# A spectral mix with its bias added by GpSimd in SBUF instead of by PE in PSUM

## The chip, the cores and the metric

The kernel runs on one core of one Trainium2 chip. A core has five engines that run side by side, each through its own instructions in order: PE (TensorE, matmuls into PSUM), VectorE (DVE), ScalarE (ACT), GpSimd (POOL) and SyncE (SP, which here issues the DMAs). They wait for each other by semaphores. The metric is device time in microseconds (us), the median of the runs shown. GpSimd reaches SBUF only; PSUM is read by VectorE and ScalarE.

## The reference, cut to what matters

```python
batch, seq, dim = 8, 3136, 256
X = np.fft.rfft(x, axis=1)                       # along the sequence
Yr = X.real @ w_r - X.imag @ w_i + b_r           # the mix, with its bias
Yi = X.real @ w_i + X.imag @ w_r + b_i
Yr = np.sign(Yr) * np.maximum(np.abs(Yr) - 0.01, 0.0)    # soft threshold, Yi alike
y = np.fft.irfft(Yr + 1j * Yi, n=seq, axis=1)
h = np.maximum(y @ w_in, 0.0)                    # then a gated feed-forward net, d_ff = 1024
gate = 1 / (1 + np.exp(-conv3(h, conv_w)))       # a 3-tap convolution along the sequence
out = (h * gate) @ w_out
```

The change touches the two lines of the mix alone: where b_r and b_i are added.

## The kernel before, in words

The sequence of 3136 is taken as 56 x 56, so that each Fourier transform is two rounds of small matmuls with tables of sines and cosines. The program has two halves. The first one (to about 580 us) makes the transform, the mix, the threshold and the first half of the inverse transform. The second one (the rest) ends the inverse transform (stage 4) and runs the feed-forward net; its instructions stand in the same order before and after the change.

The first half works on 56 groups, 7 for each of the 8 sequences, each of 4 frequencies u. One turn of its loop, for `it`, records:

- stage 2 for group it (`stage2`): eight matmuls of the second transform round, each of which PE runs as two. ScalarE copies and casts the result (tiles d and fh), VectorE makes the rest (d, fl). Numbers are kept in two parts, a high one rounded to PE's fast format (fh) and a low one (fl), so one product is three matmuls. The last piece, fl<-d,fh, reads d and fh, both in SBUF.
- the mix for group it - 1 (`mix`, named below). A complex product is made with three real products: a common one, and one for each of the two parts. The common product (ps_mx2) is copied to SBUF by ScalarE (p1, the profile's "p<-ps_mx"), and VectorE adds it to the other two (ps_mx0, ps_mx1) with four sums "v<-ps_mx,p" of 64 partitions, two per part. The threshold follows: ScalarE makes r from v, VectorE v from v and r ("v<-v,r"), ScalarE casts v to sh, and GpSimd makes the low part sl from v and sh.
- stage 3 for group it - 3 (`stage3`): 12 matmuls on sh and sl, a copy z by ScalarE and a store by SP.
- stage 1 for a later group: matmuls "ps_s<-xr,f", of which each group has two, and a copy a of each by ScalarE. For the last ten groups there is no stage 1 left.
- two pieces of background work on VectorE, which turns the feed-forward weights from double precision to two floats (the rows named win_ and wout_, later cw_): short ones with one tensor input, longer ones with two.

The bias before: two tiles, `ones` (0 but for rows 0 and 32, which are 1) and `bias` (0 but for row 0, the high part, and row 32, the low part). A matmul of `ones` with `bias` adds the bias to all 128 rows of an output. Each of the two parts has two column blocks k, so a group has four such products beside its 36 others.

The order on each engine is not the order of the code. A scheduler takes the recorded instructions, runs its own model of the engines' times, and fixes one order for each engine at build time; on the chip each engine goes through that order. The tiles that matter have few buffers: the three ps_mx tiles have one each, so that a group's products can only start when the sums of the group before have read them; sl has one, so that GpSimd waits for stage 3 of the group before; p1, v and sh have two.

Of the kernel before, what the change touches and what calls it, by code (L numbers as in the profile page):

```python
# [9 lines left out]
F32 = mybir.dt.float32  # L10
F32R = mybir.dt.float32r
I32 = mybir.dt.int32
AF = mybir.ActivationFunctionType
ALU = mybir.AluOpType
# [3 lines left out]
B, S, D, FF = 8, 3136, 256, 1024  # L18
# [6 lines left out]
UG = 4  # L25
NG = U // UG
JC = 4
P = 128
# [67 lines left out]
def spectral_ffn_kernel(ctx: ExitStack, tc: tile.TileContext, x, w_r, w_i, b_r, b_i,  # L96
                        w_in, conv_w, w_out, fwd1, fwd2, inv1, inv2, out):
    nc = tc.nc
    K1, K2 = 2 * R, 2 * SP
# [16 lines left out]
    with ExitStack() as ab:  # L116
        stg = ab.enter_context(tc.tile_pool(name="stg", bufs=1))
# [4 lines left out]
        cmx = ab.enter_context(tc.tile_pool(name="cmx", bufs=1))  # L122
# [5 lines left out]

        f1 = c1.tile([K1, P], F32, name="f1")[:, 0:K1]
        t2 = c1.tile([K1, U, K2], F32, name="t2")  # L130
        ones = cmx.tile([P, K2], F32R, name="ones")
        bias = cmx.tile([P, 2, D], F32R, name="bias")
        cmx.tile([P, 96], F32, name="pad")
        wmix_hi = cmx.tile([P, NT, 3, D], F32R, name="wmix_hi")
        wmix_lo = cmx.tile([P, NT, 3, D], F32R, name="wmix_lo")
# [3 lines left out]
        def split(dst_hi, dst_lo, src):  # L139
            nc.scalar.copy(dst_hi, src)  # L140
            nc.vector.tensor_tensor(dst_lo, src, dst_hi.bitcast(F32), op=ALU.subtract)
# [17 lines left out]

        def load_bias():  # L160

            nc.vector.memset(ones.bitcast(F32), 0.0)
            for k in (0, 32):
                nc.vector.memset(ones[k:k + 1].bitcast(F32), 1.0)
            nc.vector.memset(bias.bitcast(F32), 0.0)
            raw = stg.tile([1, 2, D], F32, name="b_raw")
            for k in range(2):
                nc.sync.dma_start(raw[:, k, :], (b_r, b_i)[k].partition_broadcast(1))
            split(bias[0:1], bias[32:33], raw)

        def load_inv1(g):
            raw = stg.tile([K2, UG, K1], F32, name="i1_raw", tag="raw", bufs=2)
# [126 lines left out]
        def mix(xs):  # L299


            fh, fl = xs
            ps = [psm.tile([K2, UG // 2, D], F32, name=f"ps_mx{c}") for c in range(3)]
            for c in (2, 0, 1):
                q = (1, 2, 0)[c]
                for k in range(UG // 2):
                    mm = [(ones, bias[:, c, :])] if c < 2 else []
                    for t in range(NT):
                        a = [f[:, t, c, 2 * k:2 * k + 2, :] for f in (fh, fl)]
                        mm += [(a[0], wmix_hi[:, t, q, :]), (a[0], wmix_lo[:, t, q, :]), (a[1], wmix_hi[:, t, q, :])]  # L310
                    for n, (lt, rh) in enumerate(mm):
                        nc.tensor.matmul(ps[c][:, k, :], lt, rh, start=(n == 0), stop=(n == len(mm) - 1))  # L312
            p1 = wk.tile([K2, UG // 2, D], F32, name="p1")
            nc.scalar.copy(p1, ps[2])
            v = wk.tile([K2, UG // 2, 2, D], F32, name="v")
            half = (slice(0, SP), slice(SP, K2))
            for c in range(2):
                for k in range(2):
                    src, dst = half[k], half[k if c == 0 else 1 - k]
                    nc.vector.tensor_tensor(v[dst, :, k, :], ps[c][src], p1[src], op=ALU.add)  # L320
            v = v.rearrange("p a b d -> p (a b) d")
            sh = wk.tile([K2, UG, D], F32R, name="sh")
            sl = wk.tile([K2, UG, D], F32R, name="sl", bufs=1)
            r = wk.tile([K2, UG, D], F32, name="r", bufs=1)
            nc.scalar.activation(r, v, AF.Relu, bias=mlam)  # L325
            thr = nc.vector.scalar_tensor_tensor(v, v, LAM, r, op0=ALU.add, op1=ALU.min)  # L326
            nc.scalar.copy(sh, v)
            SL_ENG.tensor_tensor(sl, v, sh.bitcast(F32), op=ALU.subtract)  # L328
            return sh, sl, thr
# [22 lines left out]
        p1 = NG  # L352
        load_f1()
        with tc.tile_pool(name="hx", bufs=1, reuse_waits="tile") as hx:
            xh = []
            for p in range(NG):
                xr, ld = load_x(hx, 0, p, parts=2 if p == 0 else 1, tag=f"hx{p}")
                xh.append(xr)
            with tc.issue_after(ld.ins):
                load_t2(0)  # L360
                load_mix()
                load_bias()
                st = stage1_head(xh)
        with tc.issue_after(st.ins):
# [3 lines left out]
            for i in range(2):  # L368
                a2s[i], ld = load_a2(*items[i])
        ab.enter_context(tc.issue_after(ld.ins))  # L370
        wkf, wk, cab, io = [ab.enter_context(tc.tile_pool(name=nm, bufs=n, reuse_waits="tile"))
                            for nm, n in (("wkf", 2), ("wk", 2), ("cab", 1), ("io", 2))]
# [7 lines left out]
        for it in range(n_it + 3):  # L380
            if it + 2 < n_it:
                a2s[it + 2], _ = load_a2(*items[it + 2])
            if it < n_it:
                xs[it] = stage2(items[it][1], a2s.pop(it))
            if it < NG:
                load_inv1(it)
                if it + 1 < NG:
                    load_t2(it + 1)
            if 0 <= it - 1 < n_it:
                ss[it - 1] = mix(xs.pop(it - 1))  # L390
            if 0 <= it - 3 < n_it:
                stage3(*items[it - 3], ss.pop(it - 3))
            while p1 < n_it and p1 < min(it + AHEAD, NG + 2 + it + it // 2):
                stage1(*items[p1])
                p1 += 1
            if WP0 <= it < n_it:
                with tc.issue_after(ss[it - 1][2].ins):
                    for _ in range(2 if it < LAST else 12):
                        next(background, None)


    def pool(name, bufs=1, **kw):
        return ctx.enter_context(tc.tile_pool(name=name, bufs=bufs, reuse_waits="tile", **kw))

    zio, y_a = pool("zio", 3), pool("y_a")
    wk, hp, io, y_b = pool("cwk"), pool("chp", 3), pool("cio"), pool("y_b")
# [135 lines left out]
```

## Time and profile before

| | |
|---|---|
| three runs | 1788.65, 1791.27, 1795.26 us |
| median | 1791.27 us |
| profiled execution, span | 1796.8 us |
| busy share of the span | PE 98%, VectorE 83%, ScalarE 69%, GpSimd 7% |
| first half of the program | to about 580 us, 56 groups |
| GpSimd in the first half | 56 instructions of 2.37 us |

The profiled execution is one more run of the same program; its span, from the first instruction to the last, is the only time of it that the page gives. It lies 5.5 us above the median.

How the rows read: a timeline row gives start, duration, engine, line, operation, tile written<-tiles read (buffer numbers left out), size, count and, in brackets, how long the engine stood idle before it and what ended the wait. A group row gives busy time and mean duration in ns, then idle time before the instructions and who ended it. A row of the table by stretch gives the stretch, its length, busy time and count of PE, PE's weight loads, VectorE, ScalarE and GpSimd, then the granted TensorE clock, the busy share of the DMA engines and GB/s. A row that describes one line's instructions gives minimum, median and maximum duration in ns.

### The profile page before, as it was taken

How to read it: one execution, taken by the hardware profiler on the slowest of the kernel's cores; microseconds unless marked ns; L12 is line 12 of the kernel's file. 1: busy time of each engine (PE TensorE's matmuls, PEld its weight loads, DVE VectorE, ACT ScalarE, POOL GpSimd, SP SyncE). 2: the span in 40 equal slices, each digit the busy share in tenths (PEclk: the TensorE clock that was granted, in tenths of full speed). 3: DMA queues.
4: the chain of work that ended last, by engine and by line, in shares of the span. 5: the costliest groups of instructions: out<-in, count | busy, mean ns of one | idle time of the engine just before them, and what ended most of it. 6: DMA issues, size and time to landing. Idle time of an engine off the chain costs nothing.

```text
span 1796.8 us, 29723 instructions
## 1 busy us (share of the span) xinstructions
PE 1761.6 (98%) x12320; PEld 1652.4 (92%) x12320; DVE 1484.6 (83%) x1733; ACT 1244.7 (69%) x1638; POOL 133.0 (7%) x60
## 2 busy tenths in 40 slices
PE   6999999999998999999999999999999999999999
PEld 2888989989998899999999999999999999999998
DVE  2787777787788688888888898888888888888887
ACT  2667667667665677777677777767777777767766
POOL 0122222222223000000000000000000000000000
PEclk8999999999999999999999999999999999999999
DMA  9777676676543311011011001101101111100001
GB/s 252 226 218 213 189 217 198 195 218 187 163 134 107 89 52 42 21 52 52 31 52 52 32 32 52 52 32 52 52 26 58 52 42 42 42 21 22 22 21 42
DMA packets 106810, 164.11 MB, mean 91 GB/s; under 512 B 8754, under 2 KB 85428, under 8 KB 106676
## 3 DMA queue, kind: packets, MB, share of 16 engines
q1 hardware_dynamic: 106676, 162.22, 30.2%
q8 instruction: 97, 1.59, 0.4%
q14 instruction: 37, 0.30, 0.1%
HBM read 85.13 MB, written 77.07 MB: 90 GB/s over the span
## 4 chain that ended last, share of the span: by engine, by line
PE 92%; DMA 3%; DVE 2%; ACT 1%; issue 1%; SPq 0%; ACTq 0%; DVEq 0%
PE acc L477 31%; PE ps_h L449 31%; PE ps_mx L312 12%; PE ps_s L430 5%; PE ps_s L288 5%; PE ps_s L253 4%; PE ps_s L338 4%; DVE v L320 1%; DMA wm_raw<-in_w_i_dram 1%; DMA i_raw<-in_inv_dram 1%; DMA t<-in_fwd_dram 1%; ACT r L325 0%; DMA xr<-in_x_dram 0%; DVE fl L294 0%; DMA sc<-a 0%
## 5 line engine op out<-in xcount | busy, mean ns | idle before, releaser
L477 PE MATMUL acc<-wout,gh 128*128 128x256 f32 x3136 | 567.4, 280 | 0.0
L449 PE MATMUL ps_h<-yh,win 128*128 128x450 f32 x1792 | 551.8, 368 | 1.3 <-ACT yh L436 1.2
L458 DVE SCALAR_TENSOR_TENSOR c<-h,cw,c 128x896 f32<-128x896 f32 x448 | 512.6, 1146 | 49.1 <-ACT c L456 48.1
L477 PEld LDWEIGHTS acc<-wout,gh 128*128 128x128 f32 x3136 | 493.7, 188 | 6.5
L477 PE MATMUL acc<-wout,gl 128*128 128x256 f32 x1568 | 437.6, 281 | 0.0
L451 ACT ACTIVATE h<-ps_h 128x900 f32<-128x900 f32 x224 | 207.5, 926 | 257.0 <-PE ps_h L449 256.9
L449 PEld LDWEIGHTS ps_h<-yh,win 128*128 128x128 f32 x1792 | 339.5, 189 | 27.6 <-ACT yh L436 1.4
L449 PE MATMUL ps_h<-yl,win 128*128 128x450 f32 x896 | 330.0, 368 | 0.7 <-DVE yl L437 0.7
L477 PEld LDWEIGHTS acc<-wout,gl 128*128 128x128 f32 x1568 | 293.7, 188 | 0.1
L464 DVE TENSOR_TENSOR gl<-c,gh 128x896 fp32r<-128x896 f32 x224 | 242.8, 1088 | 53.0 <-ACT gh L463 49.6
L460 DVE TENSOR_TENSOR c<-h,c 128x896 f32<-128x896 f32 x224 | 243.2, 1086 | 47.1 <-ACT c L459 46.7
L463 ACT CAST gh<-c 128x896 fp32r<-128x896 f32 x224 | 209.8, 942 | 49.3 <-DVE c L460 49.3
L459 ACT ACTIVATE c<-c 128x896 f32<-128x896 f32 x224 | 213.3, 952 | 26.4 <-DVE c L458 23.4
L312 PE MATMUL ps_mx<-wmix_hi,fh 128*128 128x256 f32 x672 | 210.0, 313 | 0.0
L312 PE MATMUL ps_mx<-wmix_hi,fl 128*128 128x256 f32 x672 | 189.3, 283 | 3.0 <-DVE fl L296 2.9
L312 PE MATMUL ps_mx<-wmix_lo,fh 128*128 128x256 f32 x672 | 189.2, 282 | 0.0
L449 PEld LDWEIGHTS ps_h<-yl,win 128*128 128x128 f32 x896 | 169.4, 189 | 12.1 <-DVE yl L437 1.0
L456 ACT ACTIVATE c<-h,cw 128x896 f32<-128x896 f32 x168 | 175.5, 1045 | 2.6
L328 POOL TENSOR_TENSOR sl<-v,sh 128x1024 fp32r<-128x1024 f32 x56 | 132.8, 2371 | 449.0 <-PE ps_s L338 382.2
L320 DVE TENSOR_TENSOR v<-ps_mx,p 64x512 f32<-64x512 f32 x224 | 154.0, 688 | 7.2 <-ACT fh L295 1.8
L326 DVE SCALAR_TENSOR_TENSOR v<-v,r 128x1024 f32<-128x1024 f32 x56 | 78.6, 1404 | 81.7 <-ACT r L325 81.6
L312 PEld LDWEIGHTS ps_mx<-wmix_hi,fh 128*128 128x128 f32 x672 | 127.0, 189 | 12.1 <-issue 11.9
(93 smaller groups left out, 2168.8 us busy)
## 6 DMA issues: line engine op xcount, KB each, us to landing
a<-sc SPq DMA_DIRECT2D x56, 448.0 KB, 5.4
sc<-z SPq DMA_DIRECT2D x56, 448.0 KB, 3.2
z<-sc SPq DMA_DIRECT2D x56, 448.0 KB, 3.9
xr<-in_x_dram SPq DMA_DIRECT2D x55, 448.0 KB, 4.2
out_dram<-o SPq DMA_DIRECT2D x27, 896.0 KB, 4.0
sc<-a SPq DMA_DIRECT2D x49, 448.0 KB, 4.4
sc<-ha SPq DMA_DIRECT2D x7, 448.0 KB, 5.5
win_bits<-in_moe_w_in_dram SPq DMA_DIRECT2D x4, 512.0 KB, 8.7
```

Source lines behind the costliest of these rows:

```text
L312: nc.tensor.matmul(ps[c][:, k, :], lt, rh, start=(n == 0), stop=(n == len(mm) - 1))
L320: nc.vector.tensor_tensor(v[dst, :, k, :], ps[c][src], p1[src], op=ALU.add)
L328: SL_ENG.tensor_tensor(sl, v, sh.bitcast(F32), op=ALU.subtract)
L449: nc.tensor.matmul(ps[:, a, 0:CH + 2], lt, rh, start=(n == 0), stop=(n == len(mm) - 1))
L451: nc.scalar.activation(h, ps[:, :, 0:CH + 2], AF.Relu)
L456: nc.scalar.mul(c, h[:, :, 0:CH], cw[:, 0, f:f + 1])
L458: nc.vector.scalar_tensor_tensor(c, h[:, :, k:k + CH], cw[:, k, f:f + 1], c, op0=ALU.mult, op1=ALU.add)
L459: nc.scalar.activation(c, c, AF.Sigmoid)
L460: nc.vector.tensor_tensor(c, h[:, :, 1:CH + 1], c, op=ALU.mult)
L463: nc.scalar.copy(gh, c)
L464: nc.vector.tensor_tensor(gl, c, gh.bitcast(F32), op=ALU.subtract)
L477: nc.tensor.matmul(acc[m // 2][:, m % 2, :], lt[:, sl], rh[:, f, :], start=(f == 0 and n == 0 and m % 2 == 0), stop=(f == NF - 1 and n == ...
```

## The change

The products with `ones` go. The bias is loaded into all 128 partitions as a plain float tile, and GpSimd makes two versions of the common product: p0 with b_r added, and p1, in place, with b_i added. The four sums on VectorE read p0 or p1 instead of p1 alone. The sums themselves, the three products and all that follows stay as they were.

```diff
-        ones = cmx.tile([P, K2], F32R, name="ones")
-        bias = cmx.tile([P, 2, D], F32R, name="bias")
+        bias = cmx.tile([P, 2, D], F32, name="bias")
...
         def load_bias():
-            nc.vector.memset(ones.bitcast(F32), 0.0)
-            for k in (0, 32):
-                nc.vector.memset(ones[k:k + 1].bitcast(F32), 1.0)
-            nc.vector.memset(bias.bitcast(F32), 0.0)
-            raw = stg.tile([1, 2, D], F32, name="b_raw")
             for k in range(2):
-                nc.sync.dma_start(raw[:, k, :], (b_r, b_i)[k].partition_broadcast(1))
-            split(bias[0:1], bias[32:33], raw)
+                nc.sync.dma_start(bias[:, k, :], (b_r, b_i)[k].partition_broadcast(P))
...
-                    mm = [(ones, bias[:, c, :])] if c < 2 else []
+                    mm = []
...
             p1 = wk.tile([K2, UG // 2, D], F32, name="p1")
             nc.scalar.copy(p1, ps[2])
+            p0 = wk.tile([K2, UG // 2, D], F32, name="p0", bufs=1)
+            pb = (p0, p1)
+            for c in range(2):
+                nc.gpsimd.tensor_tensor(pb[c], p1, bias[:, c:c + 1, :].to_broadcast([K2, UG // 2, D]), op=ALU.add)
...
-                    nc.vector.tensor_tensor(v[dst, :, k, :], ps[c][src], p1[src], op=ALU.add)
+                    nc.vector.tensor_tensor(v[dst, :, k, :], ps[c][src], pb[c][src], op=ALU.add)
```

The two DMAs of the bias keep their place in SP's queue, behind the mix's weights and ahead of the first stage-1 stores. Each now writes 128 rows of 1 KB.

The scheduler makes a new order of it. Three places follow, all from the 27th group of 56, one among many that are alike. (Lines below `load_bias` are numbered 7 less after the change, those behind the new adds 3 less.)

ScalarE, from one group's copy p1 to the next one's. Before:

```order
L314 COPY p1_3259<-ps_mx2_3218 128x512
L295 CAST fh_3193<-d_3195 128x2x256
L254 COPY a1_3177<-ps_s1_3181 112x512
L340 COPY z1_3286<-ps_s3_3273 112x1024
L325 ACTIVATE r_3268<-v_3261,small_82 128x1024
L254 COPY a1_3291<-ps_s1_3292 112x512
L291 COPY d_3305<-ps_s2_3306 128x256
L292 CAST fh_3303<-ps_s2_3306 128x512
L291 COPY d_3305<-ps_s2_3315 128x256
L292 CAST fh_3303<-ps_s2_3315 128x512
L327 CAST sh_3266<-v_3261 128x1024
L314 COPY p1_3369<-ps_mx2_3328 128x512
```

After:

```order
L307 COPY p1_3221<-ps_mx2_3184 128x512
L288 CAST fh_3159<-d_3161 128x2x256
L337 COPY z1_3251<-ps_s3_3238 112x1024
L247 COPY a1_3256<-ps_s1_3257 112x512
L322 ACTIVATE r_3233<-v_3226,small_82 128x1024
L284 COPY d_3270<-ps_s2_3271 128x256
L285 CAST fh_3268<-ps_s2_3271 128x512
L284 COPY d_3270<-ps_s2_3280 128x256
L285 CAST fh_3268<-ps_s2_3280 128x512
L324 CAST sh_3231<-v_3226 128x1024
L247 COPY a1_3256<-ps_s1_3260 112x512
L307 COPY p1_3330<-ps_mx2_3293 128x512
```

The two copies a of stage 1 moved: one now stands before r, the other between sh and the next p1. The activation r, the four instructions on d and fh, sh and the next p1 keep their order, and the cast of d (fh<-d) still comes right behind p1.

VectorE, from one threshold (v<-v,r) to the next. Before:

```order
L326 SCALAR_TENSOR_TENSOR v_3261<-v_3261,r_3268 128x1024
L194 TENSOR_SCALAR wout_e_3185<-wout_e_3185 128x512
L293 TENSOR_TENSOR d_3305<-ps_s2_3306,d_3305 128x256
L294 TENSOR_TENSOR fl_3304<-ps_s2_3306,fh_3303 128x512
L195 SCALAR_TENSOR_TENSOR wout_e_3185<-wout_bits_2518,wout_e_3185 128x512
L293 TENSOR_TENSOR d_3305<-ps_s2_3315,d_3305 128x256
L294 TENSOR_TENSOR fl_3304<-ps_s2_3315,fh_3303 128x512
L296 TENSOR_TENSOR fl_3304<-d_3305,fh_3303 128x2x256
L320 TENSOR_TENSOR v_3371<-ps_mx0_3326,p1_3369 64x2x256 x2
L320 TENSOR_TENSOR v_3371<-ps_mx1_3327,p1_3369 64x2x256 x2
L326 SCALAR_TENSOR_TENSOR v_3371<-v_3371,r_3378 128x1024
```

After:

```order
L323 SCALAR_TENSOR_TENSOR v_3226<-v_3226,r_3233 128x1024
L187 TENSOR_SCALAR wout_e_3151<-wout_e_3151 128x512
L286 TENSOR_TENSOR d_3270<-ps_s2_3271,d_3270 128x256
L287 TENSOR_TENSOR fl_3269<-ps_s2_3271,fh_3268 128x512
L286 TENSOR_TENSOR d_3270<-ps_s2_3280,d_3270 128x256
L287 TENSOR_TENSOR fl_3269<-ps_s2_3280,fh_3268 128x512
L188 SCALAR_TENSOR_TENSOR wout_e_3151<-wout_bits_2490,wout_e_3151 128x512
L289 TENSOR_TENSOR fl_3269<-d_3270,fh_3268 128x2x256
L317 TENSOR_TENSOR v_3335<-ps_mx0_3291,p0_3332 64x2x256 x2
L317 TENSOR_TENSOR v_3335<-ps_mx1_3292,p1_3330 64x2x256 x2
L323 SCALAR_TENSOR_TENSOR v_3335<-v_3335,r_3342 128x1024
```

The second piece of background work (a wout_e row here) moved from between the two halves of stage 2 to the place directly ahead of fl<-d,fh, which itself stands ahead of the four sums.

GpSimd, of which before only the rows of sl follow each other, after the change:

```order
L311 TENSOR_TENSOR p0_3223<-p1_3221,bias_115 128x512
L311 TENSOR_TENSOR p1_3221<-p1_3221,bias_115 128x512
L325 TENSOR_TENSOR sl_3119<-v_3113,sh_3118 128x1024
L311 TENSOR_TENSOR p0_3332<-p1_3330,bias_115 128x512
L311 TENSOR_TENSOR p1_3330<-p1_3330,bias_115 128x512
L325 TENSOR_TENSOR sl_3232<-v_3226,sh_3231 128x1024
```

The two adds of a group stand ahead of sl of the group before it. The second add overwrites p1, which the first one reads, so it waits for the first one's end.

## The prediction

> **What bounds the kernel now.** I read the busy shares first, then a table by stretch, then single groups of the mix stage on each engine, because the change touches that stage alone (about 50 to 580 us).
>
> ```profile
> PE 1761.6 (98%) x12320; PEld 1652.4 (92%) x12320; DVE 1484.6 (83%) x1733; ACT 1244.7 (69%) x1638; POOL 133.0 (7%) x60
> ...
> 20.00:50.00 30.00, 19.40 (x92) 13.59 (x93) 13.98 (x24) 11.65 (x24) 0.00 (x0) 0.72 1.01 266
> 300.00:400.00 100.00, 100.00 (x750) 89.61 (x749) 79.81 (x126) 70.65 (x121) 23.74 (x10) 1.00 0.71 214
> 500.00:600.00 100.00, 90.97 (x731) 88.80 (x730) 76.03 (x129) 61.17 (x88) 25.53 (x11) 0.96 0.48 134
> ```
>
> PE never rests in a mix stretch (100.00 of 100), VectorE has 20% free, ScalarE 29%, GpSimd 76%. The pace of one group is seen on PE, from one mix's first matmul to the next one's, and on GpSimd's single instruction:
>
> ```profile
> 299.95 0.37 PE L312 MATMUL ps_mx<-wmix_hi,fh 128*128 128x256 f32 x1
> ...
> 303.94 0.28 PE L312 MATMUL ps_mx<-bias,ones 128*128 128x256 f32 x1
> 304.06 0.28 PE L312 MATMUL ps_mx<-wmix_hi,fh 128*128 128x256 f32 x1
> ...
> 304.76 0.28 PE L312 MATMUL ps_mx<-bias,ones 128*128 128x256 f32 x1
> ...
> 309.56 0.37 PE L312 MATMUL ps_mx<-wmix_hi,fh 128*128 128x256 f32 x1
> 326.44 2.36 POOL L328 TENSOR_TENSOR sl<-v,sh 128x1024 fp32r<-128x1024 f32 x1 [7.24 <-PE ps_s L338]
> 336.05 2.38 POOL L328 TENSOR_TENSOR sl<-v,sh 128x1024 fp32r<-128x1024 f32 x1 [7.24 <-PE ps_s L338]
> ```
>
> A group takes 9.61 us on both. Matmuls are pipelined: a row shows 0.28 us, but from bias to bias seven starts lie 0.82 us apart, 0.117 us each. That is the price of a bias product, not its duration.
>
> **What is removed.** Four of 40 matmuls per group, 224 in all.
>
> ```profile
> L312 PE MATMUL ps_mx<-bias,ones 128*128 128x256 f32 x224 | 65.2, 291 | 1.4 <-DVE v L320 0.8 <-DVE ha L270 0.6
> L320 DVE TENSOR_TENSOR v<-ps_mx,p 64x512 f32<-64x512 f32 x224 | 154.0, 688 | 7.2 <-ACT fh L295 1.8 <-ACT p L314 1.0 <-issue 0.4
> L328 POOL TENSOR_TENSOR sl<-v,sh 128x1024 fp32r<-128x1024 f32 x56 | 132.8, 2371 | 449.0 <-PE ps_s L338 382.2 <-ACT sh L327 66.8
> L460 DVE TENSOR_TENSOR c<-h,c 128x896 f32<-128x896 f32 x224 | 243.2, 1086 | 47.1 <-ACT c L459 46.7
> L141 DVE TENSOR_TENSOR bias<-b_raw,bias 1x512 fp32r<-1x512 f32 x1 | 0.7, 681 | 0.0
> ```
>
> By the spacing the saving is 4 x 0.117 = 0.47 us a group, 26 us over 56 groups; the 65.2 us of that group's busy time count overlaps. If PE stays the bound a group takes 9.61 - 0.47 = 9.14 us. The memsets and the split of the old bias also go: the dearest of them is 0.7 us, once, at a time when PE waits for DMA (19.40 us busy of the 30 from 20 to 50 us), so I count them at nothing; were they on PE's path they would be worth under 3 us.
>
> **What is added.** Two adds of 128x512 on GpSimd per group, between the copy of the common product (ScalarE, p) and the four VectorE sums v. No row has such an add there. By half of sl's 2371 ns it is 1.19 us; it is no dearer than a whole sl, 2.37 us. VectorE's own adds give the fixed part: 693 ns (the median of fl, 512 columns, in the rows of the next fence) and 1086 ns (896 columns) are 1.02 ns a column and 0.17 us fixed. With the same fixed part, GpSimd's add is (2.37 - 0.17)/2 + 0.17 = 1.27 us, which I take, since the row of the same engine is the nearest. GpSimd's load becomes 2.37 + 2.54 = 4.9 of 9.1 us: no bound by itself.
>
> The Trainium skill, page "GPSIMD Engine Reference", section "Performance versus the Vector engine", gives 4497 ns for such an add of 2048 columns; with sl's row that makes an estimate of 1.31 us, and the sum below would be 3 us larger.
>
> **What the adds hold up.** An in-order instruction on VectorE that reads two SBUF tensors, or one in the fast form, stood still while GpSimd ran:
>
> ```profile
> 548.09 2.36 POOL L328 TENSOR_TENSOR sl<-v,sh 128x1024 fp32r<-128x1024 f32 x1 [6.78 <-PE ps_s L338]
> 548.48 2.51 DVE L296 TENSOR_TENSOR fl<-d,fh 128x512 fp32r<-128x512 f32 x1
> 551.02 1.39 DVE L320 TENSOR_TENSOR v<-ps_mx,p 64x512 f32<-64x512 f32 x2
> ...
> 538.95 2.36 POOL L328 TENSOR_TENSOR sl<-v,sh 128x1024 fp32r<-128x1024 f32 x1 [5.53 <-PE ps_s L338]
> 539.03 2.31 DVE L194 TENSOR_SCALAR cw_e<-cw_e 128x8 int32<-128x8 int32 x1
> ...
> L296 DVE TENSOR_TENSOR fl<-d,fh x56: 678/693/2783, 43.6 to 567.3; 128x512 fp32r<-128x512 f32 x56
> L320 DVE TENSOR_TENSOR v<-ps_mx,p x224: 673/689/697, 47.9 to 575.4; 64x512 f32<-64x512 f32 x112
> ```
>
> The fl that normally takes 0.69 us took 2.51 and ended at 550.99, 0.54 after GpSimd's end at 550.45. A tiny 128x8 operation took 2.31 us and ended with GpSimd's. The sums v, which read PSUM, never varied (673 to 697 ns). Now the copy p stands just ahead of the cast of d on ScalarE, so fl<-d,fh becomes ready while the first add runs; it waits for that add, and the second add then waits for fl if the hold works both ways.
>
> The Trainium skill, page "SBUF — State Buffer", section "SBUF: two separate sides", says that this port pair is an exclusive lock and that either side blocks the other for a whole instruction. The holds of VectorE agree (2.51 against 0.69 us); no row here shows GpSimd being held.
>
> **The new ring.** ScalarE, GpSimd and VectorE now form a ring from one group's r to the next one's. Its ScalarE part, from starts:
>
> ```profile
> 394.61 1.15 ACT L325 ACTIVATE r<-v,small 128x1024 f32<-128x1024 f32 x1
> 395.66 0.58 ACT L254 COPY a<-ps_s 112x512 f32<-112x512 f32 x1
> 396.13 0.39 ACT L291 COPY d<-ps_s 128x256 f32<-128x256 f32 x1
> ...
> 397.61 1.10 ACT L327 CAST sh<-v 128x1024 fp32r<-128x1024 f32 x1
> 398.56 0.63 ACT L314 COPY p<-ps_mx 128x512 f32<-128x512 f32 x1
> 395.79 1.38 DVE L326 SCALAR_TENSOR_TENSOR v<-v,r 128x1024 f32<-128x1024 f32 x1 [1.51 <-ACT r L325]
> ```
>
> r 1.05, a 0.47, d and fh twice 1.48, sh 0.95, p to its end 0.63: 4.58 us (in the new order a stands between sh and p; the sum is the same). A hand-over is 0.04 us (r ends at 395.76, VectorE starts at 395.79). Before, four sums v followed, 2.8 us: 4.58 + 2.8 + 0.08 = 7.5 us, 2.1 us inside the group's 9.61. After: first add 1.27, fl behind it 0.54, second add 1.27, the last two sums v 1.39, three hand-overs 0.12: 4.58 + 4.59 = **9.17 us**, as long as PE's 9.14. With 1.19 us an add it is 9.01 and PE binds; with 2.37 it is 11.4; at 1.49 all of the gain is gone.
>
> **The background pieces.** Weight preparation puts two pieces a group on VectorE. In 22 of the 36 groups from the 11th to the 46th (counted in the new order) the second stands directly ahead of fl<-d,fh. When it gets there, counted from r:
>
> ```profile
> 302.37 0.42 DVE L193 TENSOR_SCALAR wout_e<-wout_e 128x512 int32<-128x512 int32 x1
> 302.70 0.42 DVE L293 TENSOR_TENSOR d<-ps_s,d 128x256 f32<-128x256 f32 x1
> ...
> 388.09 0.68 DVE L207 TENSOR_TENSOR wout_m<-wout_m,wout 128x512 f32<-128x512 f32 x1
> 388.78 0.42 DVE L293 TENSOR_TENSOR d<-ps_s,d 128x256 f32<-128x256 f32 x1
> 389.12 0.68 DVE L294 TENSOR_TENSOR fl<-ps_s,fh 128x512 fp32r<-128x512 f32 x1
> 389.72 0.41 DVE L293 TENSOR_TENSOR d<-ps_s,d 128x256 f32<-128x256 f32 x1
> 390.05 0.68 DVE L294 TENSOR_TENSOR fl<-ps_s,fh 128x512 fp32r<-128x512 f32 x1
> ...
> 510.19 1.22 DVE L326 SCALAR_TENSOR_TENSOR v<-v,r 128x1024 f32<-128x1024 f32 x1
> 511.33 0.16 DVE L194 TENSOR_SCALAR cw_e<-cw_e 128x8 int32<-128x8 int32 x1
> ```
>
> v<-v,r starts 1.18 after r and, unheld, passes on after 1.14; the first piece takes 0.33 (short kind) or 0.60 (0.68 less the same overlap); d, fl, d, fl take 0.34 + 0.60 + 0.33 + 0.60. So the second piece starts at 4.52 or 4.79 us; the first add is ready at 4.62. In 6 groups (short, short) the add would wait to 4.93: ring 9.48. In 12 (short, long) to 5.20: 9.75. In 4 (long, long) the piece falls behind the add and costs 0.60: 9.77. The other 14 stay at 9.17. Against 9.61: 14 x -0.44 + 6 x -0.13 + 12 x 0.14 + 4 x 0.16 = -6.2 - 0.8 + 1.7 + 0.6 = -4.7 us. If VectorE never holds GpSimd, the 18 go at 9.17 too: -13 us.
>
> **Head and tail.**
>
> ```profile
> 507.35 2.38 POOL L328 TENSOR_TENSOR sl<-v,sh 128x1024 fp32r<-128x1024 f32 x1 [5.52 <-PE ps_s L338]
> 515.25 2.38 POOL L328 TENSOR_TENSOR sl<-v,sh 128x1024 fp32r<-128x1024 f32 x1 [5.52 <-PE ps_s L338]
> ```
>
> Near the end a group takes 7.90 us, without stage 1; there sh comes after p, out of the ring, so the five groups at that pace save 0.47 each: -2.3. Of the others I expect nothing. In the first ten the order is irregular; PE could save 4.7, ten holds of half an add (0.63) could cost 6.3: 0. The bias now lands in all partitions, 256 KB, in a stretch whose DMA is full at 266 GB/s (20 to 50 us): +1.0. Sum: -4.7 - 2.3 + 1.0 = -6.0 us, so 1796.8 becomes 1790.8 in a profile. The profiled execution lies 5.5 above the median of 1791.3; from the median the forecast is **1785 us**.
>
> **Rivals.**
> - PE stays the bound: if the hold is shorter than I think or the add cheaper than 1.25 us, all 56 groups save 0.47, 1791 - 26 = 1765 us; with the unheld case of above about 1776. For it: GpSimd is idle 76% of a mix stretch, and sl has only waited for PE. Against it: the ring sum of 9.17 has nothing to spare.
> - Slower: at the end of the first add, the second one goes ahead of the waiting fl. Then fl is done 1.27 + 0.04 later and all four sums follow: 4.58 + 0.04 + 1.27 + 0.04 + 1.27 + 0.54 + 2.8 + 0.04 = 10.6 us, +0.97 in 36 groups, +35: 1826 us. It decides wherever the second add's wait is over before VectorE gets the port. Against it: fl ended 0.54 us behind GpSimd's end, so a waiting VectorE starts at once; but no GpSimd instruction was queued there. A cheaper form of the same: an add of over 1.49 us, which at 1.6 gives 9.83 and +8 us or more.
>
> **How the numbers follow.** No measurable change (within 0.5%, 9 us, about what can be told here) 0.40; faster 0.35; slower 0.25. The range of 8 in 10 takes in most of both: 1766 to 1815; the likeliest case's own is 1782 to 1800.
>
> **What would show it.** PE's bias rows gone; a group at 9.1 to 9.8 us on the rows of sl; GpSimd adds of 1.2 to 1.3 us; fl<-d,fh at about 1.3 us median; ScalarE's r waiting for v by 2 us in every group; PE under 99% in a mix stretch. PE at 100% and groups at 9.14 would prove the ring too long in my sum; groups over 10 the slower rival. Adds far from 1.27 us upset every ring.

## The result, and the profile after

| | before | after |
|---|---|---|
| median of the runs | 1792.48 us | 1810.86 us |
| lowest and highest | 1788.65 to 1795.26 | 1807.56 to 1812.85 |
| profiled span | 1796.8 us | 1811.1 us |

Each median is of four runs; of the kernel before, a fourth run (1793.69 us) has joined the three above.

The ratio is 1.0089, with a 95% interval of 1.0065 to 1.0113. The kernel became slower by 0.9%. The forecast was "no measurable change" at 1785 us; the time lies inside the range, on the side with the smallest chance (0.25).

The busy shares of the kernel after, and its table by stretch:

```profile
PE 1748.7 (97%) x12096; PEld 1631.6 (90%) x12096; DVE 1530.8 (85%) x1728; ACT 1244.3 (69%) x1637; POOL 305.2 (17%) x172
```

```profile
300.00:400.00 100.00, 97.73 (x718) 85.93 (x716) 86.05 (x123) 68.65 (x115) 59.10 (x33) 1.00 0.72 212
500.00:600.00 100.00, 83.21 (x649) 80.21 (x649) 91.30 (x134) 60.48 (x91) 57.34 (x32) 0.95 0.37 105
```

The 224 products are gone (12320 - 12096), but PE now rests in both stretches: 97.73 instead of 100.00, and 83.21 instead of 90.97. VectorE's busy time rose by 46 us (1484.6 to 1530.8), though it does no work that it did not do before. Two descriptions of lines (minimum, median and maximum in ns) say where, and the waits say who pays:

```profile
L311 POOL TENSOR_TENSOR p<-p,bias x112: 1271/1602/2136, 48.6 to 589.8; 128x512 f32<-128x512 f32 x112
...
L289 DVE TENSOR_TENSOR fl<-d,fh x56: 678/1626/2782, 44.4 to 583.2; 128x512 fp32r<-128x512 f32 x56
```

```profile
ACT r L322 <- DVE v L317: 119.5, 48, 4.5
...
PE ps_mx L305 <- DVE fl L289: 17.0, 14, 1.9
```

The last low part, fl<-d,fh, went from a median of 693 ns to 1626. The add itself is 1271 ns where nothing disturbs it, and is stretched in its turn. ScalarE's r waits 119.5 us for the sums (48 times, 2.5 us on average; before it was 15.2 us, 10 times), and PE waits 17.0 us for fl (2.9 us before).

GpSimd's sl marks each group, so its starts divide the first half. The first, 11th, 46th and last one of before:

```profile
61.51 2.35 POOL L328 TENSOR_TENSOR sl<-v,sh 128x1024 fp32r<-128x1024 f32 x1 [61.07 <-ACT sh L327]
...
163.04 2.36 POOL L328 TENSOR_TENSOR sl<-v,sh 128x1024 fp32r<-128x1024 f32 x1 [7.25 <-PE ps_s L338]
...
499.45 2.38 POOL L328 TENSOR_TENSOR sl<-v,sh 128x1024 fp32r<-128x1024 f32 x1 [7.24 <-PE ps_s L338]
...
579.86 2.37 POOL L328 TENSOR_TENSOR sl<-v,sh 128x1024 fp32r<-128x1024 f32 x1 [2.98 <-PE ps_s L338]
```

and of after:

```profile
63.18 2.37 POOL L325 TENSOR_TENSOR sl<-v,sh 128x1024 fp32r<-128x1024 f32 x1
...
167.21 2.39 POOL L325 TENSOR_TENSOR sl<-v,sh 128x1024 fp32r<-128x1024 f32 x1
...
509.24 2.82 POOL L325 TENSOR_TENSOR sl<-v,sh 128x1024 fp32r<-128x1024 f32 x1
...
598.20 2.40 POOL L325 TENSOR_TENSOR sl<-v,sh 128x1024 fp32r<-128x1024 f32 x1 [3.82 <-PE ps_s L335]
```

In the table below, worked out from these starts, "steady" is the 35 spacings between the 11th and the 46th, "tail" the last ten.

| us | to the first sl | first ten | steady | tail | rest | span |
|---|---|---|---|---|---|---|
| before | 61.5 | 101.5 | 336.4 | 80.4 | 1216.9 | 1796.8 |
| after | 63.2 | 104.0 | 342.0 | 89.0 | 1212.9 | 1811.1 |
| difference | +1.7 | +2.5 | +5.6 | +8.6 | -4.0 | +14.3 |
| forecast | +1.0 | 0 | -4.7 | -2.3 | 0 | -6.0 |

The spans are of one execution each and lie 14.3 us apart, the medians 18.4. Before's profiled execution was a long one of its kind: its span alone is above the longest of its four runs (1795.26 us). So the 4.0 us that "rest" gives back need not come from the change.

Both large terms came out with the wrong sign. **The steady groups** are of four kinds: nine of 9.27 to 9.33 us, five of 9.57, fourteen of 9.83 to 9.86, three of 10.99 to 11.27; and two pairs with 7.7 and 12.0. Three pieces of the timeline of after show one of the fourteen, one of the three, and the second half of a pair:

```profile
338.61 0.68 DVE L192 SCALAR_TENSOR_TENSOR wout_rest<-wout_r,wout_e 128x512 f32<-128x512 int32 x1
338.62 3.51 POOL L311 TENSOR_TENSOR p<-p,bias 128x512 f32<-128x512 f32 x2 [4.00 <-ACT p L307]
339.21 1.77 DVE L289 TENSOR_TENSOR fl<-d,fh 128x512 fp32r<-128x512 f32 x1
340.90 2.81 DVE L317 TENSOR_TENSOR v<-ps_mx,p 64x512 f32<-64x512 f32 x4
...
343.81 1.15 ACT L322 ACTIVATE r<-v,small 128x1024 f32<-128x1024 f32 x1 [3.34 <-DVE v L317]
...
348.46 2.95 POOL L311 TENSOR_TENSOR p<-p,bias 128x512 f32<-128x512 f32 x2 [3.99 <-ACT p L307]
348.72 1.56 DVE L201 TENSOR_TENSOR wout<-wout_m,wout_rest 128x512 fp32r<-128x512 f32 x1
350.21 1.75 DVE L289 TENSOR_TENSOR fl<-d,fh 128x512 fp32r<-128x512 f32 x1
351.88 2.81 DVE L317 TENSOR_TENSOR v<-ps_mx,p 64x512 f32<-64x512 f32 x4
354.78 1.16 ACT L322 ACTIVATE r<-v,small 128x1024 f32<-128x1024 f32 x1 [4.48 <-DVE v L317]
...
290.98 2.35 POOL L325 TENSOR_TENSOR sl<-v,sh 128x1024 fp32r<-128x1024 f32 x1
291.12 2.76 DVE L289 TENSOR_TENSOR fl<-d,fh 128x512 fp32r<-128x512 f32 x1
```

In the first, the late background piece (338.61) runs, the first add waits for it, fl (339.21) then waits for the first add, and the second add for fl: the two adds take 3.51 us where 2.54 are their own. In the second, the piece (348.72) waits for the first add, until 348.46 + 1.27 = 349.73; when it ends, the second add goes ahead of fl, since fl is first in line only from 350.21 on. The adds end at 348.46 + 2.95 = 351.41, and fl runs only then: 10.97 us from r to r. In the third, the new order has fl behind the first two sums, 0.14 us after the start of sl, which holds it for its whole length.

**The tail** has fl behind the first two sums in four of its ten groups. One of them in full, after, from one r to the next:

```profile
512.59 1.15 ACT L322 ACTIVATE r<-v,small 128x1024 f32<-128x1024 f32 x1 [1.81 <-DVE v L317]
...
515.05 2.67 POOL L311 TENSOR_TENSOR p<-p,bias 128x512 f32<-128x512 f32 x2 [2.99 <-DVE v L323]
516.38 1.39 DVE L317 TENSOR_TENSOR v<-ps_mx,p 64x512 f32<-64x512 f32 x2
517.67 2.37 POOL L325 TENSOR_TENSOR sl<-v,sh 128x1024 fp32r<-128x1024 f32 x1
517.81 2.78 DVE L289 TENSOR_TENSOR fl<-d,fh 128x512 fp32r<-128x512 f32 x1
520.62 1.39 DVE L317 TENSOR_TENSOR v<-ps_mx,p 64x512 f32<-64x512 f32 x2
520.64 0.39 PE L305 MATMUL ps_mx<-wmix_hi,fl 128*128 128x256 f32 x1 [0.83 <-DVE fl L289]
522.05 1.15 ACT L322 ACTIVATE r<-v,small 128x1024 f32<-128x1024 f32 x1 [0.51 <-DVE v L317]
```

GpSimd starts sl directly behind the second add, 0.14 us before fl; fl stands still for all of it and takes 2.78 us instead of 0.69; and PE's next product waits for fl. The last two sums stand behind fl, so its hold lies on the way from r to r: 2.46 to the adds, 1.33 to the sums, 1.43 for two of them, 2.81 for fl, 1.43 to the next r, in all 9.46 us, where these groups took 7.90 before. With a free fl it would be about 7.4, an estimate from the same rows. Before, sl waited there for stage 3 and started at another moment; three fl were held in the tail even so, in its later groups.

Small instructions are held too. The background pieces of the tail are 128x8 and last 0.16 us; after the change ten of 27 are longer than 0.3 us (before, two were). The longest group of the tail (11.96 us) has one of them ahead of its four sums and one behind the first sum:

```profile
544.16 1.26 DVE L185 TENSOR_SCALAR cw_e<-cw_bits 128x8 int32<-128x8 int32 x1
...
545.35 2.34 POOL L325 TENSOR_TENSOR sl<-v,sh 128x1024 fp32r<-128x1024 f32 x1
546.00 1.71 DVE L189 TENSOR_SCALAR cw_m<-cw_bits 128x8 int32<-128x8 int32 x1
...
548.66 0.55 PE L305 MATMUL ps_mx<-wmix_hi,fh 128*128 128x256 f32 x1 [3.20 <-DVE v L317]
```

In the tail as a whole PE waits 8.7 us for fl (2.9 before) and 4.3 us for the sums (0.8). The stretch of these ten groups, before and after, has another difference, in the granted clock (the third number from the end):

```profile
499.45:579.86 80.41, 75.96 (x640) 74.52 (x638) 68.68 (x118) 52.34 (x80) 23.70 (x10) 1.00 0.41 117
...
509.24:598.20 88.96, 74.96 (x586) 72.85 (x586) 81.78 (x122) 52.66 (x80) 50.38 (x30) 0.94 0.37 106
```

PE runs 54 matmuls fewer here, forty of them the products, which at 0.117 us each would be 6.3 us, but it is busy only 1.0 us less. The difference may be the clock of 0.94; whether that is a cause of the late tail or comes of PE's rests, no run shows.

### The profile page after: what moved, and what is told of

It reads as the page before. It is cut to its first block, busy times and chain, and to the rows that moved or that the text cites. A ratio compares the mean times of both kernels' runs of the same rounds, so it can differ in the third digit from the quotient of the medians.

```text
span 1811.1 us, 29543 instructions
## 1 busy us (share of the span) xinstructions
PE 1748.7 (97%) x12096; PEld 1631.6 (90%) x12096; DVE 1530.8 (85%) x1728; ACT 1244.3 (69%) x1637; POOL 305.2 (17%) x172
## 4 chain that ended last, share of the span: by engine, by line
PE 76%; DVE 12%; issue 4%; ACT 4%; DMA 2%; POOL 0%; SPq 0%; ACTq 0%; DVEq 0%
PE acc L474 30%; PE ps_h L446 30%; PE ps_s L427 5%; DVE v L317 5%; PE ps_mx L305 5%; DVE fl L289 2%; PE ps_s L246 2%; PE ps_s L281 2%; PE ps_s L335 2%; DVE fl L287 1%; ACT r L322 1%; DMA i_raw<-in_inv_dram 1%; DVE d L286 1%; ACT fh L285 1%; ACT sh L324 0%
## 5 line engine op out<-in xcount | busy, mean ns | idle before, releaser
L311 POOL TENSOR_TENSOR p<-p,bias 128x512 f32<-128x512 f32 x112 | 170.9, 1526 | 279.9 <-ACT p L307 256.8
L305 PE MATMUL ps_mx<-wmix_hi,fl 128*128 128x256 f32 x672 | 193.3, 290 | 17.0 <-DVE fl L289 17.0
L305 PE MATMUL ps_mx<-wmix_lo,fh 128*128 128x256 f32 x672 | 206.1, 307 | 0.0
L305 PE MATMUL ps_mx<-wmix_hi,fh 128*128 128x256 f32 x672 | 199.0, 297 | 4.3 <-DVE v L317 4.3
L305 PEld LDWEIGHTS ps_mx<-wmix_hi,fl 128*128 128x128 f32 x672 | 128.9, 193 | 30.5 <-DVE fl L289 19.8
L322 ACT ACTIVATE r<-v,small 128x1024 f32<-128x1024 f32 x56 | 64.7, 1156 | 119.5 <-DVE v L317 119.5
```

The source lines that it names most:

```text
L311: nc.gpsimd.tensor_tensor(pb[c], p1, bias[:, c:c + 1, :].to_broadcast([K2, UG // 2, D]), op=ALU.add)
```

## The experiments

The theory: what loses the time is that fl<-d,fh, an instruction of VectorE with two inputs in SBUF, and GpSimd's instructions hold each other up. The rivals: the sums wait longer for their data, because two adds now stand between the copy p and the sums; the background pieces or the new order alone; or there was nothing to gain from the products. All are edits of the kernel after unless said otherwise. The scheduler makes a new order for each of them, so none changes one thing alone.

| us | median (ratio to before, 95% interval) | to first sl | first ten | steady | tail | rest |
|---|---|---|---|---|---|---|
| no adds | 1783.34 (0.9934, 0.9913 to 0.9955) | 58.6 | 100.2 | 322.6 | 80.5 | 1219.2 |
| adds that nobody reads | 1789.55 (0.9981, 0.9963 to 0.9999) | 61.0 | 101.6 | 336.1 | 79.0 | 1216.8 |
| adds on VectorE | 1823.38 (1.0161, 1.0144 to 1.0179) | 59.2 | 98.3 | 367.3 | 89.5 | 1212.9 |
| fl reads a PSUM tile | 1779.11 (0.9918, 0.99 to 0.9936) | 63.3 | 99.9 | 318.9 | 85.0 | 1213.8 |
| background at the end | 1836.06 (1.0237, 1.0215 to 1.0259) | 61.8 | 97.1 | 324.7 | 90.2 | 1258.3 |
| bias copied to PSUM | 1789.67 (0.9975, 0.996 to 0.9989) | 61.6 | 100.4 | 324.1 | 85.8 | 1211.9 |
| old way in the tail | 1806.60 (1.0069, 1.0048 to 1.0091) | 62.9 | 101.4 | 342.8 | 80.4 | 1216.1 |
| d in PSUM | 1774.73 (0.9895, 0.9874 to 0.9916) | 62.6 | 93.6 | 321.9 | 80.1 | 1212.6 |
| before, with d in PSUM | 1798.19 (1.0022, 1.0009 to 1.0036) | 60.3 | 100.4 | 337.2 | 81.8 | 1216.8 |
| bias copied, d in PSUM | 1791.36 (0.9981, 0.9972 to 0.9991) | 64.6 | 96.2 | 323.8 | 90.6 | 1215.6 |

The five columns on the right are of one profiled execution each. That of "adds that nobody reads" took 1796.71 us, 7.2 above its median; that of "adds on VectorE" 5.8 above, that of "bias copied to PSUM" 4.1 below; the others lie within 3.5 us of theirs.

### What there was to gain: no adds

```diff
-            p0 = wk.tile([K2, UG // 2, D], F32, name="p0", bufs=1)
-            pb = (p0, p1)
-            for c in range(2):
-                nc.gpsimd.tensor_tensor(pb[c], p1, bias[:, c:c + 1, :].to_broadcast([K2, UG // 2, D]), op=ALU.add)
+            pb = (p1, p1)
```

> The changed kernel without the two GpSimd adds; the bias is left out of the result altogether, and the four sums read the plain copy p. It shows what the removed PE products are worth by themselves. If PE is the bound of the mix stage, as the prediction had it, a group takes 9.14 us and the whole about 1792 - 26 = 1766 us. If the products were hidden in some other bound, the time stays at 1792 us or above, and the loss of the changed kernel would have nothing to do with a gain that was eaten up.

1783.34 us; the result lacks the bias. A steady group takes 9.12 to 9.15 us in all but two of the 35, which is 9.61 less the 0.47 of four products. But the tail gains nothing (80.5 against 80.4: four groups of 7.4 to 7.5, and then some of up to 10.2), and the first ten only 1.3. So leaving out the products is worth about -12 us here (0.66% of 1794), not the -26 that a saving in every group would be: PE binds in the steady part alone. It is no upper bound. In five of the last ten groups sl still holds fl (2.02 to 2.83 us), and a version below that is free of this hold is faster.

### Holds without anyone waiting for the data

```diff
-            p0 = wk.tile([K2, UG // 2, D], F32, name="p0", bufs=1)
-            pb = (p0, p1)
+            pb = (p1, p1)
...
-                nc.gpsimd.tensor_tensor(pb[c], p1, bias[:, c:c + 1, :].to_broadcast([K2, UG // 2, D]), op=ALU.add)
+                q = wk.tile([K2, UG // 2, D], F32, name=f"q{c}", bufs=1)
+                nc.gpsimd.tensor_tensor(q, p1, bias[:, c:c + 1, :].to_broadcast([K2, UG // 2, D]), op=ALU.add)
```

> As the changed kernel, but GpSimd writes its two sums into two tiles that nobody reads, and the four sums on VectorE read the plain copy p (so the bias is left out of the result). GpSimd works as before, only nobody waits for its data. If holding VectorE's two-input operations is the cause, the holds stay: fl still waits for the first add, then four sums follow, a ring of 4.58 + 0.04 + 1.27 + 0.54 + 2.8 + 0.04 = 9.27 us, and the last ten groups keep their holds by sl: 1790 to 1812 us. If the sums' waiting for the adds' data is the cause, all of it goes: about 1766 to 1772 us.

The group of fl in this run:

```profile
L289 DVE TENSOR_TENSOR fl<-d,fh 128x512 fp32r<-128x512 f32 x56 | 70.1, 1251 | 6.9 <-ACT fh L288 4.8
```

1789.55 us, 0.5 below the range expected of holds and far above that of the data. No instruction waits for these adds, and fl is held in every steady group; its mean is 1251 ns. Holding alone costs 6.2 us against no adds at all, about half of what leaving out the products gave, while the real adds cost 27.5. The steady part (336.1 in the profile, against 322.6) says more than it should: 7.4 of these 13.5 us lie in its first six groups, one of which takes 15.01 us with PE waiting 3.1 us for a DMA. The other 29 groups take 9.36 us on average, 0.21 above the 9.15 of no adds. The tail did not keep its loss, as the expectation had it: it is 79.0. So holds cost time with no one waiting for the data, but not all of it: the rest came where the held fl and the adds stand in one chain, or with the order.

### The adds on VectorE

```diff
-                nc.gpsimd.tensor_tensor(pb[c], p1, bias[:, c:c + 1, :].to_broadcast([K2, UG // 2, D]), op=ALU.add)
+                nc.vector.tensor_tensor(pb[c], p1, bias[:, c:c + 1, :].to_broadcast([K2, UG // 2, D]), op=ALU.add)
```

> The same two adds, on VectorE in place of GpSimd. No GpSimd work is added, so nothing new holds the port; the sums still wait for the adds' data, and VectorE gets 2 x 0.69 = 1.4 us a group more. If the holds are the cause, a group goes by PE or by VectorE's load, 7.6 + 1.3 = 8.9 us a group, so near 9.14 to 9.4 us: 1768 to 1785 us. If any added step between the copy and the sums costs the gain, it stays over 1792 us.

```profile
415.85 3.47 DVE L311 TENSOR_TENSOR p<-p,bias 128x512 f32<-128x512 f32 x2
415.99 2.78 POOL L325 TENSOR_TENSOR sl<-v,sh 128x1024 fp32r<-128x1024 f32 x1 [8.26 <-ACT sh L324]
...
426.01 0.68 DVE L311 TENSOR_TENSOR p<-p,bias 128x512 f32<-128x512 f32 x1
426.03 2.88 POOL L325 TENSOR_TENSOR sl<-v,sh 128x1024 fp32r<-128x1024 f32 x1 [7.27 <-ACT sh L324]
426.61 2.85 DVE L289 TENSOR_TENSOR fl<-d,fh 128x512 fp32r<-128x512 f32 x1
```

1823.38 us, far from what I expected, and by its time on the side of the rival. But eleven steady groups, with the added step in them, ran at 9.13 to 9.17 us, as forecast; the later ones at 10.0 to 11.6, more than half of them at 11.0. The rows are of two such groups: the adds, now VectorE's own, also have two inputs in SBUF, and sl starts beside the first of them. The second add is then held (two take 3.47 us, a free one 0.68), or fl is, with 2.85 us. I had left sl on GpSimd out of the sum, as in the prediction. Those eleven groups and these rows speak for holds, but since the run made new ones its time can't tell the theories apart.

### fl without its second SBUF input

```diff
-            nc.vector.tensor_tensor(fl[:, :, 2], d, fh[:, :, 2].bitcast(F32), op=ALU.subtract)
+            nc.vector.tensor_tensor(fl[:, :, 2], ps.rearrange("p (t a) c m -> p t (a c) m", t=NT), fh[:, :, 2].bitcast(F32), op=ALU.subtract)
```

> The changed kernel, but the operation fl<-d,fh reads a PSUM tile of the same size in place of d (so its numbers are wrong). It has one SBUF input then, as the sums v have, which were never held. The adds and the waits for their data are all there. If the hold of fl is the cause, fl takes 0.69 us in every group, and the ring falls to 4.58 + 0.04 + 1.27 + 0.05 + 1.27 + 0.04 + 1.39 + 0.04 = 8.7 us, below PE's 9.14; background pieces are still held: 1770 to 1790 us. If the wait for the adds' data is the cause, it stays at 1805 us or above.

fl in this run, by its line:

```profile
L289 DVE TENSOR_TENSOR fl<-ps_s,fh x56: 674/691/693, 44.2 to 550.3; 128x512 fp32r<-128x512 f32 x56
```

1779.11 us, 32 us less than the kernel after, by one operand. fl never varies now (674 to 693 ns). The adds and the sums that wait for them are still there, and the steady part takes 318.9 us, with PE busy all of the time. This is the run that decides against the data: waiting for it costs little as long as fl isn't held. How much of the 32 us is the hold itself stays open, since the order is another one in the steady part too (the late background piece stands between the halves of stage 2 again, as before the change). The tail stays long (85.0): there the small pieces are still held, seven of 27 for over 0.3 us and up to 2.32, and PE's longest wait (3.51 us, for the sums) comes behind two of them.

### The background pieces taken out

```diff
-                    for _ in range(2 if it < LAST else 12):
-                        next(background, None)
+                    if it == n_it - 1:
+                        for _ in background:
+                            pass
```

> The changed kernel, with the background pieces (the weight preparation on VectorE) taken out of the loop and recorded after the last group. If the uneven groups (9.57, 9.84, 10.99 us) come from a piece that stands ahead of fl<-d,fh, then every group from the 11th to the 45th takes the 9.3 us of the groups without such a piece: 35 groups in 325 to 328 us where the changed kernel needed 342.0. If instead the adds alone, or the order of GpSimd, make them uneven, the mean stays above 9.6 and the stretch above 336. The whole run gets longer in either case, since about 100 pieces of 0.4 to 0.7 us, and the casts and loads they need, then stand alone between the two halves: 1830 to 1870 us.

1836.06 us with the pieces behind the last group, and a steady part of 324.7 us: 28 of the 35 spacings of sl lie between 9.28 and 9.34, and none reaches 9.5. So the pieces made the kinds of 9.57, 9.84 and 11 us. The ring (from one r to the next, over ScalarE, GpSimd and VectorE) stands undisturbed in this run:

```profile
336.22 1.15 ACT L322 ACTIVATE r<-v,small 128x1024 f32<-128x1024 f32 x1 [2.20 <-DVE v L317]
...
340.18 0.62 ACT L307 COPY p<-ps_mx 128x512 f32<-128x512 f32 x1
340.87 2.98 POOL L311 TENSOR_TENSOR p<-p,bias 128x512 f32<-128x512 f32 x2 [4.00 <-ACT p L307]
341.35 1.37 DVE L289 TENSOR_TENSOR fl<-d,fh 128x512 fp32r<-128x512 f32 x1 [0.74 <-ACT fh L288]
342.64 2.80 DVE L317 TENSOR_TENSOR v<-ps_mx,p 64x512 f32<-64x512 f32 x4
345.54 1.15 ACT L322 ACTIVATE r<-v,small 128x1024 f32<-128x1024 f32 x1 [2.19 <-DVE v L317]
```

r to the end of p: 4.58 us (340.80 - 336.22). From there: hand-over 0.07, first add 1.27 to 342.14, fl behind it 0.50, four sums without a gap 2.80, hand-over 0.10. Sum 4.58 + 4.74 = 9.32 us.

### The tail in the old way

`mix` gets a switch that adds the bias with products on PE and leaves the adds out, for the last eleven groups:

```diff
-                    mm = []
+                    mm = [(ones, biasp[:, c, :])] if pe and c < 2 else []
...
-            for c in range(2):
+            for c in range(0 if pe else 2):
...
-                ss[it - 1] = mix(xs.pop(it - 1))
+                ss[it - 1] = mix(xs.pop(it - 1), it - 1 >= 45)
```

> The changed kernel, with the last eleven groups done as before the change: bias products on PE, no adds on GpSimd. If the tail's 8.6 us are lost because sl, which now starts right behind the second add, holds fl<-d,fh, then the ten groups from the 46th on go back from 89.0 to 80 to 82 us and the run is 7 to 9 us shorter than the changed kernel: 1802 to 1804 us. If the tail is late for another reason (the order on ScalarE and VectorE that the groups before hand on, or the lower clock), it stays at 86 or more and the time at 1808 or more.

The tail is back at 80.4 us, all of the 8.6, while the steady part stays as slow (342.8). The profiled executions differ by 7.5 us, but the medians by 4.3 only (1806.60), not the 7 to 9 expected; in the profile the rest of the program takes 3.2 us longer (1216.1 against 1212.9). So the adds in these groups, with the order that they bring, cost the tail; the timeline rows above show holds as the way. The granted clock of the tail is back at 1.00 too, so the rival of a lower clock is not parted from the holds by this run.

### Two versions in which no add can hold fl

The first one, in which ScalarE copies the bias into PSUM and the products add to it:

```diff
+            for c in range(2):
+                nc.scalar.copy(ps[c], bias[:, c:c + 1, :].to_broadcast([K2, UG // 2, D]))
...
-                        nc.tensor.matmul(ps[c][:, k, :], lt, rh, start=(n == 0), stop=(n == len(mm) - 1))
+                        nc.tensor.matmul(ps[c][:, k, :], lt, rh, start=(c == 2 and n == 0), stop=(n == len(mm) - 1), skip_group_check=True)
...
-                nc.gpsimd.tensor_tensor(pb[c], p1, bias[:, c:c + 1, :].to_broadcast([K2, UG // 2, D]), op=ALU.add)
```

> No product for the bias on PE and no add on GpSimd: ScalarE copies the bias from SBUF into the two PSUM tiles ahead of the products, which add to it. VectorE's four sums read p as before the change, so no instruction holds the port but sl. If the port is what ate the gain, PE is the bound again at 9.14 us a group: 35 groups in 320 to 324 us and 1765 to 1785 us in all. The rival: the copies (2 of 0.63 us a group) stand between the sums of one group and the products of the next, since each ps_mx tile has one buffer, so PE waits for them: groups over 9.6, 1795 us or more.

1789.67 us, between the two expectations: the steady part is at 324.1, near PE's bound (35 x 9.14 = 320), but the tail at 85.8. The second one keeps the adds, and puts d into PSUM:

```diff
-                nc.vector.tensor_tensor(d[:, t], psv[:, 0], d[:, t], op=ALU.subtract)
                 nc.vector.tensor_tensor(fl[:, t, 0:2], psv, fh[:, t, 0:2].bitcast(F32), op=ALU.subtract)
-            nc.scalar.copy(fh[:, :, 2], d)
-            nc.vector.tensor_tensor(fl[:, :, 2], d, fh[:, :, 2].bitcast(F32), op=ALU.subtract)
+                nc.vector.tensor_tensor(psv[:, 1], psv[:, 0], d[:, t], op=ALU.subtract)
+                nc.scalar.copy(fh[:, t, 2], psv[:, 1])
+                nc.vector.tensor_tensor(fl[:, t, 2], psv[:, 1], fh[:, t, 2].bitcast(F32), op=ALU.subtract)
```

> The changed kernel with its two adds, but the difference d is written into PSUM, over the half of ps_s that has been read, so that the last low part fl and its cast fh read PSUM (in two halves of 256 columns). fl then has one SBUF input and is not held. If the hold of fl is the cause of the loss, this does what the run with a wrong input for fl did, with every number in place: 35 groups in 318 to 326 us, 1777 to 1790 us. If stage 2's PSUM tiles, which are now freed about 3 us later, make PE wait, or the two halves cost ScalarE and VectorE more than the hold did, it is 1800 us or more.

Its groups, and its table by stretch:

```profile
L311 POOL TENSOR_TENSOR p<-p,bias 128x512 f32<-128x512 f32 x112 | 150.8, 1346 | 262.2 <-ACT p L307 153.0 <-DMA t<-in_fwd_dram 48.2 <-DVE fl L286 19.1
...
L289 DVE TENSOR_TENSOR fl<-ps_s,fh 128x256 fp32r<-128x256 f32 x112 | 45.6, 420 | 8.9 <-ACT fh L288 6.1
```

```profile
300.00:400.00 100.00, 100.00 (x745) 89.11 (x745) 86.25 (x142) 75.54 (x133) 56.00 (x33) 1.00 0.71 210
```

1774.73 us: 1.05% faster than before (0.84% to 1.26%), and the fastest of all. PE is at 100.00 again, a steady group at 9.20 us (321.9 / 35), the tail at 80.1, though small pieces are still held there. The same move without the change answers whose gain that is:

> The kernel before (bias products on PE, no adds), with the difference d in PSUM as in the run before it. If that run is faster because the four products are gone and nothing holds fl any more, then d in PSUM alone changes nothing here, since PE is the bound: 9.61 us a group, 336 us for 35 groups, 1788 to 1796 us. If d in PSUM is the gain by itself, this kernel is as fast as that one, 1772 to 1780 us.

1798.19 us, 2 us over the range expected, and 9.63 us a group: d in PSUM is worth nothing (0.2% the other way) while PE is the bound. So the gain is not the move's alone; it needs the products gone. How the 1.05% divides is not shown: no adds without the move gave 0.66%, and no run has no adds and the move. The last run put d into PSUM in the version with the copied bias:

> The kernel in which ScalarE copies the bias into PSUM ahead of the products, with the difference d in PSUM too. GpSimd then does sl alone and nothing on VectorE in this stage that PE waits for can be held. If holds of fl by sl are what the last ten groups of that kernel lose (85.8 us), they come to 80 here, and the run to 1776 to 1784 us. If ScalarE's load (over 84% busy with the copies) is what they lose, it stays at 1785 us or more.

Its waits of PE between 500 and 556 us:

```profile
PE ps_mx L307 <- ACT ps_mx L298: 5.4, 8, 1.2
PE ps_s L281 <- DVE fl L289: 3.2, 2, 1.6
```

1791.36 us, and a tail of 90.6: the expectation that holds of fl cost that version its tail falls, since no fl is held here. PE waits there for ScalarE's copies of the bias, 8 times, and for low parts. So a late tail can have other causes than holds.

## Why the prediction was wrong

**The prices were right.** Four products are 0.47 us (9.61 to 9.14 without them). The add is 1.271 us at its shortest, for which the prediction had 1.27 with a fixed part borrowed from VectorE. The part from r to the end of p is 4.58 in both. The hold works both ways: the add has a median of 1602 ns and goes up to 2136. The Trainium skill, page "SBUF — State Buffer", section "SBUF: two separate sides", has the lock between a GpSimd instruction and a VectorE one with two SBUF inputs: the one that starts first has the shared pair of ports for its whole instruction, and the other one waits. The prediction had rows for one direction; the add's 1602 ns agree for the other, and so does the fl that reads PSUM, at 674 to 693 ns.

**The largest failure is the tail**, 10.9 us off (-2.3 forecast, +8.6 measured). The step was "there sh comes after p, out of the ring, so the five groups at that pace save 0.47 each". It took sh out of the ring and looked no further. What it missed is that fl stands between the sums there, and that the change moves sl: behind two adds in GpSimd's order, it starts when the second add ends, which here is when fl comes up. The prediction costed fl against the adds, never against sl, though its own rows had an sl that held an fl for 2.51 us; and it put the 128x8 pieces at nothing, though its rows had one held for 2.31 us. The rows of after show both holds, 2.78 us for fl and up to 1.71 for a piece. With the old way in the tail, the 8.6 us are gone. How they divide between fl, the pieces and the clock of 0.94 stays open.

**The steady groups** are 10.1 us off: the prediction's four kinds give 331.9 us for 35 groups (its 36 make 341.3), and 342.0 were measured.
- The ring of 9.17 is 9.32. The term that was mis-sized is "second add 1.27": the first two sums run beside it and last 1.39, so the four sums take 2.80 where I had 1.27 + 1.39 = 2.66; fl is 0.04 shorter and the hand-overs are 0.05 more. The kinds with a late piece shift in the same way: 9.57 for 9.48, 9.84 for 9.75. Together about 3 us.
- "In 4 (long, long) the piece falls behind the add and costs 0.60: 9.77" measured 10.99 to 11.27, three times, 4 us. The piece does fall behind the first add; but then the second add goes ahead of fl. This is the mechanism of the slower rival, which I had priced at 10.6 at the end of the first add in every group. It decides only where a piece stands between.
- The remaining 3 us are in the main the two pairs in which fl was put behind the first two sums and met sl. The prediction classed the groups by the late piece and not by this.

**The head** is 3.2 us off (+4.2 against +1.0). Its groups are irregular without any adds too (17.75 us in one place there, 18.36 after), and no run takes it apart. **The rest** of the program gave back 4.0 us that the forecast did not have. The granted clock of the stretch from 580 to 700 us, 0.96 before and 0.99 after, would make 0.03 x 120 = 3.6 us of it; but the kernel before with d in PSUM had 0.99 there as well, and a rest of 1216.8 us like before's 1216.9. So the cause is open, and with one execution of each it may be no effect of the change at all.

**The rivals.** "PE stays the bound" gave 1776 us for the case that VectorE never holds GpSimd. The two runs with the adds on GpSimd in which fl can't be held measured 1779.11 and 1774.73. No run came down to the full 1765: even without any adds it is 1783.34, since head and tail did not gain what PE was spared. The slower rival came true in three of 35 groups only. That the time lies inside the stated range is luck: neither of the two ways to its slow end, a second add ahead of fl in every group or an add of 1.6 us by itself, is what happened.

**The signs named** came in part: r waits for v in every steady group, PE is under 99% in a mix stretch, most groups lie between 9.1 and 9.8 us or just above. Two spoke against the forecast: fl was to have a median of about 1.3 us and had 1.63, and the adds were to take 1.2 to 1.3 us and had a median of 1.60, because they are held too.

## What to carry to other kernels

When work goes to GpSimd, list every VectorE instruction that can meet it and be held (two inputs in SBUF, but here 128x8 pieces with one input too), and every instruction of GpSimd that the new one moves; in this tail the price was less the length of the added work than the moment at which the instruction behind it now starts. Where a low part or a difference can stay in PSUM, an operand there takes the instruction out of the contest: the change that cost 0.9% gained 1.05% with that one move and the order that came of it. It is no gift by itself: it gained nothing where PE was the bound, nor in the version with the copied bias (1791.36 against 1789.67 us). And price each engine's part of a ring by what ends last there, sum by sum: two sums beside an add are as long as the longer of the two.

## What the runs showed of the hardware

- Who goes first. When a VectorE instruction already waits as an add ends, it goes ahead of the add queued behind (fl in the steady groups); when the add already waits as a VectorE instruction ends, the add goes ahead of the next VectorE instruction (348.46 to 351.41 us above). In these rows, the turn went to the one that had waited.
- At their shortest, an add of 128x512 on GpSimd is 1271 ns and sl, twice as many columns, 2338: nearly proportional, with about 0.2 us fixed (2 x 1.271 - 2.338), an estimate that takes the two operations to cost alike.
- The length of a hold does not go by the size of what is held: a 128x8 piece of 0.16 us took up to 1.71 us beside sl, and shows as a longer instruction, not as a wait.
- One operand in PSUM instead of SBUF made 32 us of difference in 1811 (fl's median: 691 against 1626 ns), with no instruction more or less but with another order on the engines.
